# Five transposes for two token tiles, a 40-column state readout and a new hand-written order in a fused mixer kernel

## The chip, the cores and the metric

The kernel runs on 1 core of one Trainium2 chip. The metric is the device time in microseconds (us) of one execution. Before the change it is 473.45 us (median of 3 runs, 473.36 to 474.95).

## What is computed

Three blocks follow each other, for 4 batches, 768 tokens and 320 channels (8 heads of 40). The first is a gated linear-attention recurrence, done in the kernel by chunks of 128 tokens. The second is a gated convolution block. The third adds the real part of a 2-D Fourier transform, normalises each token and applies a two-layer network:

```
C = f*C + i*outer(v, k);  n = f*n + i*k          # per token, per head, 40 x 40
y = sigmoid(o) * (C @ q) / max(|n . q|, 1)
gate = sigmoid(causal_conv5(x));  x = (gate * (x @ w_val)) @ w_out
u = x + real(fft(fft(x, tokens), channels))
un = (u - mean(u)) / sqrt(var(u) + 1e-6)          # over the 320 channels of a token
out = u + relu(un @ w_ch1) @ w_ch2                # 320 -> 1280 -> 320
```

## The kernel before

The program first writes down every instruction as a unit (a run of matmuls into one output tile counts as one unit, each other instruction as its own) and then issues the units in the order of a list, `ORDER` (L44). `CELL` (L142) gives each buffer its slot, and `FILLS` (L173) puts dummy matmuls on a constant tile ahead of named units, as (unit, how many, PSUM bank). Each engine and the SP queue, which issues nearly all DMAs, works strictly in the order in which the list names its units. There is no planner at run time.

For each batch b the units come from these functions, c being one of six chunks, i one of three pairs of token tiles (one tile from each half hf of the sequence):

- `prologue_gates` (L433) and `a_fb`, `a_pre`: the gates, their decay factors d (a scan on VectorE, DVE) and the scaling of k, v and q. The gate rows are turned on TensorE (PE) with the constant `pat`, which arrives by DMA.
- `s_mm`, `u_mm` (L680), `a_u` (L693), `a_pv` (L718), `a_fin` (L754), `a_tr` (L778): scores, the state update u, the carried state cc, the read of state and values (e times cc, d times v), the division by max(|n.q|,1), and the transpose of the result. In batches 1 to 3 `a_pv` joins the scores, the e-times-cc matmuls, the u of the next chunk and the d-times-v matmuls. The first d-times-v matmul waits for an empty instruction on the SP queue, which itself waits for the last e-times-cc matmul.
- `u_mm` works in 64 x 64 quarters of the PE array: for each pair of heads p, each half chunk x and each head s, the weights are 64 columns of k from column 40h on, of which only the first 40 belong to head h. The last chunk has one x instead of two.
- `p_conv`, `p_val`, `p_g`, `p_z`, `p_fold`, `b_s`, `b_se`, `b_d` (L950), `b_de` (L961): convolution block and Fourier transform.
- `b_ln` (L980): mean and variance on DVE, the power -0.5 on GpSimd (POOL), then two ScalarE (ACT) instructions that write the two normalised tiles `un` of 320 columns. `b_ut` (L1011), called twice (L1127): three PE transposes of one tile (`tr3`, L773, columns 0 to 127, 128 to 255 and 192 to 319, so that 64 columns are turned twice), one ACT copy to `uH`, and two DVE subtractions that write the low part `uL` and the copy that lies in the other 64 partitions.
- `m_1` (L1028) and `m_2` (L1045): the two layers of the network, in 16 and 6 matmuls at a time. The low part `hl` of the hidden layer is written by DVE between them.
- Weights arrive as raw 64-bit numbers and are turned into 32-bit ones by four DVE instructions each (`to_f32`, L496, tile `mk`), in the order list spread over the work of batch 0 and the start of batch 1.

PE's list runs through batch 0 up to its normalisation, fills 23 dummy matmuls in, and then starts the first `m_1`; from there on the network of one batch stands between the attention and transform work of the next.

```
            m = slice(256 * n + 128 * q, 256 * n + 128 * q + 128)
            for k in range(2):
                ops += [(w1H[:, k, m], uH[:, k]), (w1H[:, k, m], uL[:, k]), (w1L[:, k, m], uH[:, k])]
            ops += [(w1T[:, m], uH[:, 2]), (w1U[:, m], uH[:, 2])]
```

Of the kernel before, what the change touches and what calls it, by code (L numbers as in the profile page):

```python
# [12 lines left out]
AF = mybir.ActivationFunctionType  # L13
# [25 lines left out]
NCC = 4  # L39
FB0 = 4  # L40
# [131 lines left out]
]  # L172
FILLS = [  # L173
    (78, 4, 1), (82, 8, 3), (30, 1, 0), (203, 5, 3), (262, 10, 5), (220, 2, 1), (427, 2, 1), (485, 5, 0), (512, 23,
    1), (540, 2, 1), (544, 1, 1), (1023, 2, 2),
]

# [1062 lines left out]
```

## Time and profile before

| | us |
|---|---|
| median of 3 runs | 473.45 |
| the profiled execution's own time | 474.57 |
| span of the profiled execution, first to last instruction | 472.5 |
| PE busy | 453.3 |
| DVE busy | 332.6 |
| ACT busy | 183.5 |
| POOL busy | 162.0 |

The profile gives for each engine its busy time, in 40 slices and in any stretch asked for, with the clock that PE was granted as a share of full speed (1.00 is 2.4 GHz, 0.50 is 1.2 GHz). Matmuls overlap in PE's pipeline, so the price of one in a dense run is the distance between starts, not its duration. PE weight loads (PEld) run beside the matmuls.

### The profile page before, as it was taken

To read this page: it belongs to the slowest core of one execution; us is meant where nothing else is said; L and a number is where in the kernel's file an instruction comes from. 1 tells how busy PE (TensorE), PEld (TensorE's weight loads), DVE (VectorE), ACT (ScalarE), POOL (GpSimd) and SP (SyncE) were. 2 spreads that over 40 slices of the span, in tenths; PEclk is the share of its full clock that TensorE was granted. 3 is DMA by queue.
4 is the path that set the end of the run, shared out by engine and by line. 5 is a ranking of instruction groups with operands and counts; after the bars stand their busy time and mean duration, and the time that the engine had idled before them with its cause. 6 is when DMAs were issued, how large, how long until landed. Compare 5 with 4: busy or idle time off the path is not lost.

```text
span 472.5 us, 13916 instructions
## 1 busy us (share of the span) xinstructions
PE 453.3 (96%) x5798; PEld 425.6 (90%) x5798; DVE 332.6 (70%) x810; ACT 183.5 (39%) x414; POOL 162.0 (34%) x210
## 2 busy tenths in 40 slices
PE   7998989898999989999999999999999999999996
PEld 7887767787999989889999899899999998999996
DVE  5867888899969669587568686596697683763131
ACT  5653355544334235435224254244233432342120
POOL 4554355824664331601443443122534121010000
PEclk8959999999999999999999999999999999999999
DMA  7688544634532162101330542001310000000000
GB/s 204 192 228 218 143 123 139 216 96 140 140 105 69 47 170 79 42 17 43 90 111 2 158 146 70 1 2 60 99 57 17 1 30 1 28 1 1 28 29 28
DMA packets 23301, 39.84 MB, mean 84 GB/s; under 512 B 4752, under 2 KB 14288, under 8 KB 23240
## 3 DMA queue, kind: packets, MB, share of 16 engines
q1 hardware_dynamic: 23192, 38.90, 27.6%
q8 instruction: 45, 0.74, 0.7%
q14 instruction: 16, 0.13, 0.1%
q0 software_dynamic: 48, 0.07, 0.1%
HBM read 32.77 MB, written 4.23 MB: 78 GB/s over the span
## 4 chain that ended last, share of the span: by engine, by line
PE 73%; DVE 15%; DMA 4%; ACT 3%; issue 2%; SPq 1%; POOL 1%; DVEq 0%; ACTq 0%; POOLq 0%
PE bank L300 73%; DVE mk L300 2%; DVE bank L300 2%; DVE z L300 2%; DVE d L300 2%; DMA exr<-in_c_ex_dram 1%; SPq L300 1%; DVE bs L300 1%; DMA scr<-fh 1%; DMA kvo<-in_kvo_dram 1%; DMA wvU<-tl 1%; DVE r L300 1%; DMA dmat<-in_c_d_dram 1%; DVE e L300 1%; POOL eo L300 1%
## 5 line engine op out<-in xcount | busy, mean ns | idle before, releaser
L300 PE MATMUL bank<-uu,w1H 128*128 128x256 f32 x480 | 93.2, 286 | 0.6 <-ACT gate L300 0.2
L300 PEld LDWEIGHTS bank<-uu,w1H 128*128 128x128 f32 x480 | 74.7, 188 | 2.6 <-DVE uu L300 0.8
L300 PE MATMUL bank<-w2H,hh 128*128 128x320 f32 x240 | 74.8, 319 | 0.0
L300 PE MATMUL bank<-w2L,hh 128*128 128x320 f32 x240 | 72.3, 309 | 0.0
L300 ACT ACTIVATE hh<-bank 128x512 fp32r<-128x512 f32 x60 | 35.8, 596 | 85.9 <-PE bank L300 82.7
L300 PE MATMUL bank<-uu,w1L 128*128 128x256 f32 x240 | 67.3, 281 | 0.0
L300 DVE SCALAR_TENSOR_TENSOR hl<-bank,hh 128x512 fp32r<-128x512 f32 x60 | 40.8, 686 | 27.3 <-ACT hh L300 26.6
L300 PE MATMUL bank<-w2H,hl 128*128 128x320 f32 x240 | 55.1, 310 | 1.4 <-DVE hl L300 1.4
L300 DVE SCALAR_TENSOR_TENSOR bank<-xT,cw,bank 128x384 f32<-128x384 f32 x84 | 48.3, 618 | 1.6 <-ACT bank L300 0.8
L300 PEld LDWEIGHTS bank<-w2H,hh 128*128 128x128 f32 x240 | 45.1, 188 | 1.0 <-issue 0.3
L300 PEld LDWEIGHTS bank<-w2L,hh 128*128 128x128 f32 x240 | 45.2, 188 | 0.3
L300 PEld LDWEIGHTS bank<-uu,w1L 128*128 128x128 f32 x240 | 45.2, 188 | 0.0
L300 DVE TENSOR_TENSOR z<-z,bank 128x161 f32<-128x161 f32 (+2 forms) x76 | 26.5, 377 | 21.9 <-PE bank L300 21.2
L300 PEld LDWEIGHTS bank<-w2H,hl 128*128 128x128 f32 x240 | 40.1, 188 | 1.9 <-DVE hl L300 1.9
L300 POOL TENSOR_TENSOR gL<-gg,gH 128x384 fp32r<-128x384 f32 x16 | 16.7, 1048 | 60.7 <-ACT gH L300 60.7
L300 POOL TENSOR_TENSOR cc<-cc,fcol 128x164 f32<-128x164 f32 x40 | 21.8, 544 | 36.5 <-DVE cc L300 15.7
L300 PE MATMUL bank<-uu,w1T 128*128 128x256 f32 x120 | 33.7, 281 | 0.0
L300 PE MATMUL bank<-uu,w1U 128*128 128x256 f32 x120 | 33.7, 281 | 0.0
L300 DVE TENSOR_TENSOR_SCAN d<-bank,pat 128x512 f32<-128x512 f32 x24 | 29.0, 1216 | 4.7 <-PE bank L300 4.5
L300 POOL TENSOR_TENSOR kvo<-kvo,r 128x320 f32<-128x320 f32 x24 | 17.5, 731 | 40.9 <-DVE r L300 35.3
L300 POOL TENSOR_TENSOR r<-ve,mhalf 128x2 f32<-128x2 f32 x12 | 8.3, 695 | 56.5 <-DVE ve L300 45.6
L300 POOL TENSOR_TENSOR kvo<-kvo,d 128x320 f32<-128x320 f32 x24 | 18.3, 762 | 24.5 <-DVE d L300 22.5
(153 smaller groups left out, 1047.9 us busy)
## 6 DMA issues: line engine op xcount, KB each, us to landing
kvo<-in_kvo_dram SPq DMA_DIRECT2D x24, 484.0 KB
qk<-in_qk_dram SPq DMA_DIRECT2D x48, 160.0 KB
raw<-in_w_dram SPq DMA_DIRECT2D x9, 640.0 KB
out_dram<-z SPq DMA_DIRECT2D x24, 160.0 KB
e<-sce SPq DMA_DIRECT2D x30, 80.0 KB
cs<-in_c_cs_dram SPq DMA_DIRECT2D x2, 386.0 KB
raw<-in_w_val_dram SPq DMA_DIRECT2D x1, 640.0 KB
raw<-in_w_out_dram SPq DMA_DIRECT2D x1, 640.0 KB
```

The source lines that it names most:

```text
L300: i = getattr(engine, method)(*a, **k)
```

## The change

- **Transposes.** For batches 1 to 3 the two normalised tiles of a pair are written side by side into one tile `up` of 640 columns (three ACT instructions instead of two), and five transposes of 128 columns turn all of it. The ACT copies and DVE subtractions behind it change from two and four to four and four.
- **Readout.** `u_mm` loads 40 weight columns instead of 64 and writes 40 partitions of each half instead of 64.
- **Warm-up.** The twelve dummy matmuls at the start write to six banks instead of one.
- **Order, slots and fills.** `ORDER`, `CELL` and `FILLS` are new. There are 71 dummy matmuls instead of 65.

```diff
+PAIR = (1, 2, 3)
 FILLS = [
-    (78, 4, 1), (82, 8, 3), (30, 1, 0), (203, 5, 3), (262, 10, 5), (220, 2, 1), (427, 2, 1), (485, 5, 0), (512, 23,
-    1), (540, 2, 1), (544, 1, 1), (1023, 2, 2),
+    (25, 2, 2), (45, 15, 0), (283, 5, 6), (267, 5, 6), (220, 10, 6), (427, 1, 1), (485, 3, 1), (544, 26, 3), (516, 1,
+    0), (576, 1, 6), (652, 2, 0),
 ]
...
-        for _ in range(WARM):
-            nc.tensor.matmul(out=banks()[:, 7, 0:L], lhsT=a, rhs=a, start=True, stop=True)
+        for n in range(WARM):
+            m = L * (n // 6)
+            nc.tensor.matmul(out=banks()[:, n % 6, m:m + L], lhsT=a, rhs=a, start=True, stop=True)
...
-                    T.matmul(out=u[64 * s:64 * s + 64, x, p, :], lhsT=t["kvo"][r, D * h:D * h + LS], rhs=t["vp"][r, h],
+                    T.matmul(out=u[64 * s:64 * s + D, x, p, :], lhsT=t["kvo"][r, D * h:D * h + D], rhs=t["vp"][r, h],
...
+        pair_ = wt("up", [128, 2 * DM], "U") if b in PAIR else None
+        if pair_ is not None:
+            un[b, i, "p"] = pair_
         for hf in range(2):
+            nrm = dict(scale=r0[:, hf:hf + 1], bias=nb[:, hf:hf + 1])
+            if pair_ is not None:
+                z = zt[b, hf, i]
+                for o, n in ((0, ((0, 320),)), (320, ((64, 256), (0, 64))))[hf][1]:
+                    k = (0, 320) if hf == 0 else ((0, 256) if n == 256 else (256, 320))
+                    A.activation(pair_[:, 320 * hf + o:320 * hf + o + n], z[:, k[0]:k[1]], AF.Identity, **nrm)
+                continue
             u = wt("un", [128, DM], "C")
-            A.activation(u, zt[b, hf, i], AF.Identity, scale=r0[:, hf:hf + 1], bias=nb[:, hf:hf + 1])
+            A.activation(u, zt[b, hf, i], AF.Identity, **nrm)
...
+    def b_ut2(b, i, _):
+        u = un.pop((b, i, "p"))
+        uH, uL = un[b, i]
+        for hf in range(2):
+            tp = mm("tp", [128, 3 - hf, L])
+            for j in range(3 - hf):
+                x = u[:, 384 * hf + 128 * j:384 * hf + 128 * j + 128]
+                T.matmul(out=tp[:, j, :], lhsT=x, rhs=ident, is_transpose=True, start=j == 0, stop=True,
+                         skip_group_check=True)
+            ss = slice(hf * L, hf * L + L)
+            A.activation(uH[:, 0:2, ss], tp[:, 0:2], AF.Copy)
+            V.tensor_tensor(uL[:, :, ss], tp[:, 0:2], f(uH[:, 0:2, ss]), op=ALU.subtract)
+            if hf == 0:
+                for n in range(2):
+                    r, w, sn = slice(64 * n, 64 * n + 64), slice(64 - 64 * n, 128 - 64 * n), slice(n * L, n * L + L)
+                    A.activation(uH[r, 2, sn], tp[r, 2], AF.Copy)
+                    V.tensor_tensor(uH[w, 2, sn], tp[r, 2], f(uH[r, 2, sn]), op=ALU.subtract)
```

The order list, some 2,000 numbers, is told here by its places that matter. A name such as u:0:1 is the step, the batch and the chunk (or pair); FILL15 stands for 15 dummy matmuls.

```
PE, start of the program
  before  gates FILL4 fb:0:1 fb:0:0 gates FILL8 pre:0:1 u:0:0 FILL1 gates(fm 1) fb:0:2 pre:0:0
          s0:0 gates(fm 2) u:0:1 pv:0:0 pre:0:3 pv:0:1
  after   s0:0 FILL2 gates fb:0:1 fb:0:0 fb:0:2 pre:0:1 gates(fm 1) pre:0:0 gates u:0:0 FILL15
          gates(fm 2) u:0:1 pv:0:0 pv:0:1 pre:0:2 pre:0:3
SP queue, start of the program (DMAs)
  before  gi gf qk qk pat kvo exr conv_w qk conv_w kvo qk epat conv_w conv_w kvo w_val ...
  after   gf conv_w conv_w conv_w gi conv_w qk qk pat kvo kvo epat qk w_val qk exr kvo ...
DVE, between the reciprocal and the product x of chunk 0, batch 0
  before  nothing
  after   one mk instruction, e:0:2, a reciprocal
DVE, between the two state sums cc of chunk 2, batch 0
  before  nothing
  after   one mk instruction, xH:0:0, d:0:4
PE, batch 0, normalisation to network
  before  FILL23 ut:0:0 fb:1:0 ut:0:0 FILL2 ut:0:1 FILL1 ut:0:1 m1:0:0
  after   FILL26 ut:0:1 ut:0:1 FILL1 ut:0:0 ut:0:0 s0:1 FILL1 m1:0:0
DVE, ahead of the last uu of pair 0 of batch 0: in the new order also
  the four uu of pair 1, two short steps of pair 2's normalisation, and the last of the conversion of
  one 640-column weight tile (1 instruction) and all of one 320-column tile (4 instructions)
PE, batch 1, from the first d to the first m1
  before  d:1:0 m2 d:1:2 d:1:1 fb:2:0 m2 m2 m2 m2 ut:1:0 ut:1:0 FILL2 m1:1:0
  after   d:1:0 fb:2:0 d:1:0 d:1:2 m2 m2 d:1:1 m2 s0:2 m2 ut2:1:0 (two tiles) ut2:1:0 (three) fb:2:1 m1:1:0
SP queue, batch 1, just ahead of the empty instruction of chunk 4
  before  gate rows, out, k/v/o of batch 3 chunk 4, out
  after   out, e, e, qk, qk, out, gate rows
```

## Rows read from the trace of the kernel before

**Rows 1.** Page, parts 1 and 2: busy us and share; granted clock in 40 slices.

```profile
PE 453.3 (96%) x5798; PEld 425.6 (90%) x5798; DVE 332.6 (70%) x810; ACT 183.5 (39%) x414; POOL 162.0 (34%) x210
...
PEclk8959999999999999999999999999999999999999
```

**Rows 2.** Windows: from:to, length, then busy us and count per engine, clock, DMA.

```profile
0.00:22.50 22.50, 18.31 (x270) 16.97 (x272) 15.50 (x30) 13.93 (x27) 12.80 (x21) 0.92 0.68 194
22.50:35.50 13.00, 12.74 (x235) 11.65 (x230) 9.14 (x24) 7.40 (x24) 6.18 (x8) 0.50 0.80 233
35.50:47.00 11.50, 9.88 (x209) 8.97 (x208) 9.00 (x19) 4.18 (x12) 5.50 (x8) 0.95 0.86 221
47.00:107.50 60.50, 55.83 (x593) 46.02 (x592) 53.72 (x138) 30.16 (x69) 30.44 (x33) 0.98 0.47 140
107.50:168.00 60.50, 57.71 (x1006) 55.23 (x1007) 49.51 (x100) 22.34 (x45) 29.95 (x33) 1.00 0.36 107
168.00:468.50 300.50, 298.53 (x3499) 286.76 (x3497) 195.21 (x501) 105.53 (x241) 77.08 (x108) 1.00 0.16 49
```

**Rows 3.** Waits of PE from 107.5 us on: us in total, times, longest.

```profile
PE bank L300 <- DVE hl L300: 1.5, 2, 1.4
PE bank L300 <- SPq L304: 1.0, 1, 1.0
```

**Rows 4.** Timeline of PE: start, us; runs of nine and of three transposes of un.

```profile
421.22 1.15 PE L300 MATMUL bank<-pat,un 128*128 128x128 f32 x9
...
432.03 0.49 PE L300 MATMUL bank<-pat,un 128*128 128x128 f32 x3
```

**Rows 5.** Timeline of PE, batch 2: e times cc, u, d times v.

```profile
234.24 0.63 PE L300 MATMUL bank<-cc,e 40*64 40x41 f32 x32
234.68 0.66 PE L300 MATMUL bank<-kvo 64*64 64x41 f32 x32
235.15 0.66 PE L300 MATMUL bank<-kvo,d 64*64 64x41 f32 x32
...
266.55 0.66 PE L300 MATMUL bank<-kvo 64*64 64x41 f32 x16
```

**Rows 6.** Groups of weight loads by form: busy us, mean ns, idle before.

```profile
L300 PEld LDWEIGHTS bank<-cs,eo 128*128 128x128 f32 x64 | 10.4, 189 | 2.0 <-POOL eo L300 1.1 <-issue 0.8
...
L300 PEld LDWEIGHTS bank<-cs,eo 128*64 128x64 f32 x64 | 5.0, 136 | 1.3 <-issue 0.5 <-ACT kvo L300 0.2 <-DVE os L300 0.2
```

**Rows 7.** Timeline of ACT and PE, batch 1, pair 0: un, transposes, first m1.

```profile
208.56 1.20 ACT L300 ACTIVATE un<-z,nb,r 128x320 f32<-128x320 f32 x2 [1.53 <-DVE nb L300]
209.85 1.04 ACT L300 ACTIVATE uu<-bank 128x384 fp32r<-128x384 f32 x2
...
209.26 1.09 PE L300 MATMUL bank<-pat,un 128*128 128x128 f32 x6
...
210.94 0.84 PE L300 MATMUL bank<-uu,w1H 128*128 128x256 f32 x2
```

**Rows 8.** Timeline of DVE: its two longest waits, 22 to 47 us.

```profile
29.42 0.49 DVE L300 TENSOR_TENSOR x<-bank,kvo 128x320 f32<-128x320 f32 x1 [2.20 <-POOL kvo L300]
...
39.82 0.33 DVE L300 TENSOR_TENSOR cc<-cc,bank 128x164 f32<-128x164 f32 x1 [2.04 <-POOL cc L300]
```

**Rows 9.** Groups of DVE by form: conversions mk and split uu; busy us, mean ns.

```profile
L300 DVE SCALAR_TENSOR_TENSOR mk<-raw,mk 128x640 int32<-128x640 int32 x22 | 19.0, 862 | 0.2
...
L300 DVE TENSOR_TENSOR uu<-bank,uu 128x256 fp32r<-128x256 f32 x24 | 10.0, 420 | 5.3 <-ACT uu L300 5.1
...
L300 DVE TENSOR_TENSOR uu<-bank,uu 64x128 fp32r<-64x128 f32 x24 | 6.6, 291 | 1.3 <-ACT uu L300 0.9
...
L300 DVE SCALAR_TENSOR_TENSOR mk<-raw,mk 128x320 int32<-128x320 int32 x6 | 4.2, 700 | 0.1
```

**Rows 10.** Timeline of PE: its waits for pat and for the second fm, batch 0.

```profile
7.89 0.28 PE L300 MATMUL bank<-pat,gi 32*128 32x32 f32 x2 [1.97 <-DMA pat<-in_c_pat_dram]
...
21.38 0.48 PE L300 MATMUL bank<-fm,epat 32*128 32x128 f32 x2 [1.17 <-DVE fm L300]
```

More of the change, by code (lines that the diff above doesn't have):

```diff
@@ L1125, in mixer_kernel @@
             run("ln", b_ln, b, i)
-            for hf in range(2):
+            if b in PAIR:
+                run("ut", b_ut2, b, i, 0)
+            for hf in range(0 if b in PAIR else 2):
                 run("ut", b_ut, b, i, hf)
```

251 rows, old and new, of tables (CELL, ORDER) are left out of this document.

## The prediction

> **What bounds the kernel now.** I read the page first and then cut the span into stages by windows. PE is busy 96% of the span and DVE 70% [rows 1], but that is an average over two regimes. From 168 us on PE is busy 298.53 of 300.50 us while DVE is busy 195.21; there only PE's own work counts, and at most 1.97 us of gaps can be won [rows 2]. From 107.5 to 168 us PE lacks 60.50 - 57.71 = 2.79 us; the waits that end there are one for DVE's `hl` (1.4 of 1.5 us) and one for the empty SP instruction (1.0 us) [rows 3]. Before 107.5 us, where the first network matmul of batch 0 starts, DVE sets the pace: from 47 us it is busy 53.72 of 60.50 us. In the first 47 us it is idle 7.00 + 3.86 + 2.50 = 13.4 us, waiting for DMAs, POOL and a PE that had half its clock from 22.5 to 35.5 us [rows 2]. PE's busy time there says little, since dummy matmuls count as busy.
>
> So the end of the program is the start of the first `m_1` (107.5 us), plus PE's work after it, plus PE's gaps after it. I cost the change by these three. The profiled run took 474.57 us, 2.1 more than its span and 1.1 more than the median of 473.45; the sum is made against 474.57.
>
> **Transposes.** Nine pairs lose one transpose each. Nine in a row take 1.15 us and three take 0.49, so one costs (1.15 - 0.49) / 6 = 0.11 us [rows 4]. All nine lie in the PE-bound stage: 9 x 0.11 = -1.0 us. If a change of operand eats as much as it frees the gain is 0, and it can't be over 1.0. ACT gets one more normalising instruction and two more copies per pair; ACT is busy 105.53 of 300.50 us there [rows 2], so their work is hidden, except where PE waits for the pair, below. DVE keeps four subtractions.
>
> **Readout.** A group of 32 u-instructions starts 0.47 us before the next kind of matmul, and a group of 16, which uses two of the four quarters of the array, takes the same 0.66 us from start to end [rows 5]. So the pace is set by the quarter: 0.47 us / 8 = 0.058 us for each slot of a quarter, not by the number of instructions. That the slot is the weight load is likely from the loads of one operand: 128 columns take 189 ns, 64 take 136, which is 0.83 ns a column [rows 6]. Twenty-four columns fewer are then 20 ns a slot and 8 x 20 = 0.16 us a group. Batches 1 to 3 have 18 groups: at most -2.9 us, at least 0. But 15 of them are what PE does while the SP queue answers the wait ahead of d times v; a shorter group uncovers part of it. I take 0.10 us a group, -1.8 us. Batch 0's groups lie in the DVE-paced stage and give nothing.
>
> The trace paces these matmuls at 0.47 / 32 = 15 ns. The Trainium skill (TensorE: Matmul & The Clock Gate, "Wait — 56ns, not 53.3ns?") says that starts never come closer than about 25 ns however narrow the matmul; by that rule fewer columns would give nothing at all. The trace contradicts the figure, but a floor of its own close to 15 ns isn't excluded, and that case is a rival.
>
> **The pair's chain in batch 1.** Now the first `un` is ready at about 209.2 us, the transposes start at 209.26 and the first `m_1` at 210.94 [rows 7]. In the new order the first transposes are those of the second tile, which need two of the three ACT instructions, and the last three need all: 1.20 us of ACT plus a short third one, instead of 0.6. The PE work between the first `d` and these transposes is a little less than now, and behind them only one `fb` matmul stands ahead of `m_1`, with the copies and subtractions in between (1.04 us of ACT for both tiles now, rows 7). I take +1.2 us, once; from 0 to +2.1. In batches 2 and 3 the lists put one to three `m_2` groups behind the transposes, which cover it.
>
> **Gaps after 107.5 us.** Together they are 4.8 us. The SP wait of 1.0 us goes, because in the new order the output DMA that stood right ahead of the empty instruction, and the DVE step that it waits for, have been moved up. Of the `hl` wait I let half go: conversions that DVE did between the first `uu` and the first `hl` now stand before, but others come in. I take -1.5; the bounds are -4.8 and, as a new list can open gaps of its own, +2.
>
> **The start, to the first `m_1`.** DVE must do more before it: four `uu` of pair 1 (2 x 0.42 + 2 x 0.29 = 1.42), one `mk` of 640 columns (0.86) and the conversion of a 320-column tile (2 x 0.70 and two shorter), at least 3.7 us [rows 9]. Against that, DVE's two longest stalls are given work: between the reciprocal and x (2.20 us, behind POOL) and between two state sums (2.04 us, behind POOL) stand now other DVE steps [rows 8]. That is -4.2. FILL15 keeps PE busy during the wait for the second `fm` (1.17 us), after which PE fell to half its clock for 13 us [rows 10, 2]; with full clock the rest of DVE's 6.4 idle us from 22.5 to 47 could go too. On the other side `pat` goes from fifth to ninth place in the SP queue, and PE already waits 1.97 us for it [rows 10]; the FILL4 that now follows it is gone, so I let these cancel. I take -0.5; from -6.4 + 3.7 = -2.7 to +3.7.
>
> The longer block of dummy matmuls ahead of the transposes (26 for 23) costs nothing as long as DVE's chain is later than PE. The warm-up's six banks cost nothing: the matmuls are the same and PE runs them in order. All other moves of the lists are taken as inside the bounds above.
>
> **Sum.** -1.0 - 1.8 + 1.2 - 1.5 - 0.5 = -3.6 us: 471.0 for an execution like the profiled one, 469.8 at the median.
>
> **The rivals.** *PE keeps its clock at the start.* All 6.4 us of DVE idle go, and most gaps and the whole readout gain come: -1.0 - 2.9 + 1.2 - 3.5 - 2.7 = -8.9, 464.6. For it speaks FILL15 at the very place where PE fell idle; against it, that from 22.5 to 35.5 us the DMA engines are 80% busy too [rows 2]. *The readout gives nothing*, by a floor on starts: 469.8 + 1.8 = 471.6, inside 0.5%. For it: no row shows a quarter-array matmul with fewer weight columns than 64, so a floor just below 15 ns would stay unseen; against it, as far as the trace goes: the group of 16 that takes as long as the group of 32 [rows 5]. *The gains cancel*: the stalls at the start go but the gaps stay, and batch 1 costs 2.1: 473.45 - 1.0 - 1.8 + 2.1 - 0.5 = 472.3. *Slower: the first layer starts late.* The mechanism is DVE's queue ahead of the first `m_1`. If the two POOL stalls come back elsewhere in the first 47 us, the 3.7 us stand, PE idles behind them, and the later gaps don't close because DVE owes the same sum by the end of batch 1: 473.45 + 3.7 - 1.0 - 1.0 + 1.2 = 476.4 us. It decides from the point where less than 1.5 of the 4.2 us of stalls is won. For it speaks that DVE's sum ahead of that point is surely larger; against, that the same conversions no longer stand between the first `uu` and the first `hl`.
>
> **How the numbers follow.** Forecast 0.40, clock kept 0.15, readout nothing 0.12, gains cancel 0.15, slower 0.18. A measurement tells this kernel from no change at about 0.5%, 2.4 us: below 471.1 is faster, above 475.8 slower. That gives faster 0.55, same 0.27, slower 0.18. The range of 8 in 10 runs from the clock case with its own spread, 463.5, up to the slower case, 476.0.
>
> **What would show it.** Transposes of the pairs fall from 54 to 45 at an unchanged 0.11 us. The u group should start 0.30 to 0.37 us before d times v instead of 0.47. The windows should give a first `m_1` between 105 and 108 us; a start beyond 110 us with DVE idle in the first 47 us still over 12 us would be the slower case. A granted clock of 1.00 from 22 to 36 us would be the faster one. The wait for the empty SP instruction should be gone; if it appears 15 times at 0.1 us, the readout uncovered it. In batch 1, PE should be idle for about 1 us ahead of the pair's first `m_1`. I would be wrong if PE's gaps after 168 us grew beyond 2 us, or if the first layer's start moved by more than 4 us either way.

## The result and the profile after

The changed kernel takes 477.45 us (median of 14 runs, 475.78 to 482.94), the kernel before 473.81 us in runs on the same chip: a ratio of 1.0059, 95% interval 1.0030 to 1.0087. It is slower by 0.6%. The forecast was 469.8 us, with 463.5 to 476.0 as range, so the prediction was wrong in sign and the time lies outside the range. The ratios and their intervals are taken from fast runs alone (the 482.94 was a slow one), so they aren't the quotients of the medians. The profiled execution of the changed kernel took 478.08 us.

The first rows are from the page of the changed kernel (busy us, share, count; clock in 40 slices), to be read against [rows 1]. PE is busy 4 us less than before and the span is 3.6 us longer: the parts have taken work off PE, and idle time has taken its place.

```profile
PE 449.3 (94%) x5801; PEld 421.5 (89%) x5801; DVE 327.3 (69%) x810; ACT 187.3 (39%) x441; POOL 159.5 (34%) x210
...
PEclk8887999999999999999999989999999999999999
```

The windows of the changed kernel, over the stretches of [rows 2] (from:to, length, busy us and count of PE, PEld, DVE, ACT, POOL, then clock, DMA share, GB/s):

```profile
0.00:22.50 22.50, 18.98 (x242) 17.95 (x242) 16.19 (x31) 13.03 (x23) 11.60 (x19) 0.85 0.68 199
22.50:35.50 13.00, 8.72 (x261) 7.60 (x259) 8.23 (x22) 5.29 (x15) 8.13 (x11) 0.88 0.67 205
35.50:47.00 11.50, 10.11 (x195) 8.93 (x195) 8.85 (x17) 4.70 (x14) 6.05 (x8) 0.69 0.72 205
47.00:107.50 60.50, 54.99 (x599) 46.38 (x600) 51.79 (x134) 30.29 (x74) 28.81 (x33) 1.00 0.56 158
107.50:168.00 60.50, 58.62 (x926) 55.93 (x925) 46.79 (x107) 24.70 (x53) 25.47 (x31) 1.00 0.33 99
168.00:468.50 300.50, 294.11 (x3562) 281.16 (x3561) 194.49 (x502) 109.26 (x266) 79.49 (x112) 0.99 0.16 48
```

Two losses stand here. The first `m1` of batch 0 starts at 112.40 us instead of 107.54, with a little more work done by then; what that is worth is taken up behind the experiments. And from 168 us on PE was idle 1.97 us before [rows 2] and is idle 6.39 us now. PE's waits in that stretch name the places (us in total, times, longest):

```profile
PE bank L302 <- POOL kvo L302: 2.2, 1, 2.2
PE bank L302 <- ACT xT L302: 1.4, 1, 1.4
PE bank L302 <- ACT uu L302: 0.8, 1, 0.8
PE bank L302 <- DVE nb L302: 0.6, 1, 0.6
```

**The wait of 1.4 us.** SP, ACT and PE around 248 us (start, us, engine, instruction, in brackets the idle time before it and what ended it):

```profile
243.82 0.36 SPq L302 DMA_DIRECT2D kvo<-in_kvo_dram  x1
...
247.89 0.47 ACT L302 ACTIVATE kvo<-kvo 128x320 f32<-128x320 f32 x1 [2.80 <-DMA kvo<-in_kvo_dram]
248.27 0.47 ACT L302 ACTIVATE xT<-bank 128x384 f32<-128x384 f32 x1
...
248.79 0.50 PE L302 MATMUL bank<-uu,w1H 128*128 128x256 f32 x2 [1.42 <-ACT xT L302]
```

SP issues the load of k, v and o of chunk 5 of batch 2 at 243.82 us. ACT's sigmoid of that chunk waits for it until 247.89, 2.80 us in which ACT has other work but may not start it: the copy `xT` of an earlier chunk stands behind the sigmoid in ACT's list. PE's next `m1` is to use the bank that `xT` reads. So PE waits for a load that no matmul near it needs.

**The wait of 2.2 us.** The same on POOL, 25 us later:

```profile
266.92 0.36 SPq L302 DMA_DIRECT2D kvo<-in_kvo_dram  x1
...
270.79 1.27 POOL L302 TENSOR_TENSOR e<-e,qk 128x512 f32<-128x512 f32 x1 [2.26 <-DMA e<-sce]
272.39 0.73 POOL L302 TENSOR_TENSOR kvo<-kvo,isT 128x328 f32<-128x328 f32 x1 [0.34 <-DMA kvo<-in_kvo_dram]
273.09 0.73 POOL L302 TENSOR_TENSOR kvo<-kvo,d 128x320 f32<-128x320 f32 x1
...
273.88 0.46 PE L302 MATMUL bank<-kvo 64*40 64x41 f32 x13 [2.21 <-POOL kvo L302]
```

The instruction for which PE waits is the product of `kvo` and `d` at 273.09, chunk 5 of batch 2. Ahead of it on POOL stand a product for the row tile `e` of that chunk, which waited 2.26 us for its own DMA, and a scaling by `isT` that belongs to chunk 2 of batch 3 and whose load was issued at 266.92. PE needs neither yet.

Finer windows show the stage where this falls. Of the kernel before, then of the changed one:

```profile
205.00:240.00 35.00, 34.59 (x520) 32.66 (x519) 26.14 (x80) 12.00 (x25) 11.70 (x18) 1.00 0.21 64
240.00:264.00 24.00, 24.00 (x392) 23.16 (x391) 18.42 (x38) 8.66 (x19) 8.42 (x12) 1.00 0.21 68
264.00:290.00 26.00, 25.11 (x331) 24.14 (x330) 19.02 (x41) 11.95 (x28) 10.62 (x13) 1.00 0.45 140
```

```profile
205.00:240.00 35.00, 33.74 (x513) 31.23 (x512) 26.93 (x84) 14.27 (x37) 10.40 (x16) 1.00 0.16 45
240.00:264.00 24.00, 22.58 (x355) 21.67 (x357) 16.85 (x35) 8.76 (x19) 5.52 (x8) 1.00 0.11 37
264.00:290.00 26.00, 23.68 (x363) 22.68 (x351) 14.93 (x35) 8.58 (x22) 9.22 (x12) 0.93 0.48 138
```

From 205 to 290 us PE's idle time goes from 1.30 to 5.00 us. And behind the 2.2 us wait the granted clock is 0.93 over 26 us, where it was 1.00; at 0.07 of the stretch that is another 1.8 us at most.

### The profile page after: what moved, and what is told of

Same layout as the page of the kernel before. It is cut to its first block, busy times and chain, and to the rows that moved or that the text cites. A ratio compares the mean times of both kernels' runs of the same rounds, so it can differ in the third digit from the quotient of the medians.

```text
span 476.1 us, 13939 instructions
## 1 busy us (share of the span) xinstructions
PE 449.3 (94%) x5801; PEld 421.5 (89%) x5801; DVE 327.3 (69%) x810; ACT 187.3 (39%) x441; POOL 159.5 (34%) x210
## 4 chain that ended last, share of the span: by engine, by line
PE 78%; DVE 9%; DMA 5%; issue 2%; ACT 2%; POOL 1%; SPq 1%; DVEq 0%; ACTq 0%; POOLq 0%
PE bank L302 77%; DMA kvo<-in_kvo_dram 3%; DMA qk<-in_qk_dram 2%; SPq L302 1%; PE bank L358 1%; DVE z L302 1%; DVE d L302 1%; DVE bank L302 1%; DVE uu L302 1%; POOL eo L302 1%; DVE bs L302 1%; POOL kvo L302 1%; DVE mk L302 1%; ACT uu L302 1%; DVE x L302 0%
## 5 line engine op out<-in xcount | busy, mean ns | idle before, releaser
L302 POOL TENSOR_TENSOR cc<-cc,fcol 128x164 f32<-128x164 f32 x40 | 20.6, 514 | 44.5 <-DVE cc L302 21.6
L302 POOL TENSOR_TENSOR kvo<-kvo,isT 128x328 f32<-128x328 f32 x24 | 18.4, 771 | 25.7 <-DMA kvo<-in_kvo_dram 22.6
```

The lines of the kernel that those rows point to most:

```text
L302: i = getattr(engine, method)(*a, **k)
```

## The experiments

Steps are named as in the order list above; u:2:4 is step u of batch 2, chunk 4. Each ratio is to runs of the kernel before on the same chip.

The theories were: **A**, the parts gain and the new order loses it at the start, where the first `m1` came at 112.4 instead of 107.5 us; **B**, it is lost in batch 2, at the two waits; **C**, the parts themselves gain nothing or cost.

### Each part in the old order, and the old start

**e1**: the kernel before with the 40-column readout and the six-bank warm-up.

```diff
-                    T.matmul(out=u[64 * s:64 * s + 64, x, p, :], lhsT=t["kvo"][r, D * h:D * h + LS], rhs=t["vp"][r, h],
+                    T.matmul(out=u[64 * s:64 * s + D, x, p, :], lhsT=t["kvo"][r, D * h:D * h + D], rhs=t["vp"][r, h],
```

> The kernel before with the 40-column readout (and the warm-up over six banks that it needs) and nothing else: order, buffers and fills as they were. Theory A (the two parts gain what was forecast, the new order of the start loses more): about 1.8 us less than the kernel before, 472.0 us at its median of 473.8. Theory C (the narrower readout gains nothing, since the starts of those matmuls have a floor): within 0.5 us of the kernel before.

Measured: 473.67 us, ratio 0.9970 (0.9939 to 1.0000). A gain of 0.3%, between the two theories, with an interval that just reaches no gain. Its trace shows a place where some of it was lost again. PE and SP of e1 at 165 us, and the window behind:

```profile
164.86 0.75 SPq L300 DMA_DIRECT2D out_dram<-z  x1
...
165.72 0.68 PE L300 MATMUL bank<-kvo,d 64*64 64x41 f32 x32 [1.61 <-SPq L304]
...
166.00:176.00 10.00, 9.84 (x138) 9.39 (x131) 5.24 (x15) 3.09 (x8) 3.85 (x5) 0.83 0.48 144
```

The output store in the first line stands on SP right ahead of the empty instruction for which PE waits. That wait, 1.0 us before [rows 3], has grown to 1.61, and the clock of the next 10 us is 0.83. This was followed up in e11 and e14.

**e2** and **e3**: five transposes in the old order, each step of a pair where the old steps stood; e2 with 64 columns, e3 with 40.

```diff
-PE   ut:b:i:0 (three transposes)  ut:b:i:1 (three)      ACT  un un  uu uu
+PE   ut2:b:i (three)  ut2:b:i (two)                     ACT  up up up  uu uu uu uu
```

> The kernel before with five instead of six transposes in batches 1 to 3 and nothing else: each step of a pair stands where the old steps stood, and the readout keeps 64 columns. Theory A: 1.0 us less for nine transposes and up to 1.2 us more where the first pair of batch 1 waits for both of its normalisations, so 472.8 to 474.0 us beside 473.8. Theory C: 474 us or more, since the transposes lie beside waits and two more evictions by ACT and one more subtraction by DVE come on each pair.

> Both parts in the old order, with the old fills and, but for 20 buffers, the old buffers. Theory A: the sum of the two, 471.0 to 472.2 us beside 473.8, so some 5 to 6 us less than the changed kernel. Theory B (the parts and the start matter little; the late loads of batch 2 lose it): about 473.8 less 1 to 2 us as well, so this run tells only the parts' own worth. Theory C: 474 us or more.

Measured: 484.57 us, ratio 1.0209 (1.0177 to 1.0241), and 482.41 us, ratio 1.0160 (1.0124 to 1.0197). Both lie above the 474 us of theory C, and by far more than its reasons give. PE's waits from 168 us on in e2:

```profile
PE bank L306 <- DVE uu L306: 5.3, 5, 1.9
```

Five waits for DVE's subtractions. In the longest, the first `m1` of batch 1 was to write a bank that the last subtraction of the pair had just read; the new slots had been handed out without regard to that. So these two runs don't price the pairs; e10 and e13 repeat them.

**e4**: the changed kernel, but everything up to the transforms of batch 1 issued in the order of the kernel before, with its fills and slots there.

```diff
-ORDER  new order
+ORDER  the first 956 steps of the old order, then all others as the new order has them
```

> The changed kernel, with all that it has, but its work up to the transforms of batch 1 (about 205 us) is issued in the order of the kernel before; from there on in its own order. Theory A (the start loses 3.5 to 4.9 us: the first m1 at 112.4 instead of 107.5 us): 472.5 to 474 us, first m1 back at 107 to 108 us. Theory B (what is lost is lost in batch 2, where two loads come late and PE stands 1.4 and 2.2 us with a lower clock behind; an earlier start is waited away there): 476 to 477.5 us, near the changed kernel's 477.45, with both waits still there and longer.

Measured: 490.01 us, ratio 1.0310 (1.0270 to 1.0350). Both theories missed: beside the two waits (1.85 and 1.73 us here) a third came, 5.35 us ahead of the transform of batch 2. It is of their kind:

```profile
302.90 0.99 SPq L306 DMA_DIRECT2D kvo<-in_kvo_dram  x2
...
309.36 0.83 ACT L306 ACTIVATE kvo<-kvo 128x320 f32<-128x320 f32 x2 [3.53 <-DMA kvo<-in_kvo_dram]
...
312.63 1.90 PE L306 MATMUL bank<-dmat,w 128*1 128x161 f32 x5 [5.35 <-DVE w L306]
```

ACT's copies `od` stand behind two sigmoids, which wait 3.53 us for loads issued at 302.90; DVE's `w` waits for `od`, and PE for `w`. One line of e4 speaks on theory A. The first `m1` of the pair of batch 1, in e4 and then in the changed kernel:

```profile
214.41 0.85 PE L306 MATMUL bank<-uu,w1H 128*128 128x256 f32 x2 [0.80 <-ACT uu L306]
```

```profile
214.41 0.84 PE L302 MATMUL bank<-uu,w1H 128*128 128x256 f32 x2 [0.81 <-ACT uu L302]
```

The old start brought batch 1 no sooner to this point, by which both have issued the same matmuls but for the dummies. In e4 the first `m1` came at 108.0 us, 4.4 sooner, but from there PE was idle 4.9 us instead of 2.0, and it had more left to do: ahead of its first `m1` the new order has also issued the scores and the state update of one chunk (64 matmuls, 1.0 us). These are single executions, and the start varies. The same start list in the changed kernel, in e5 and in e9 (below):

```profile
112.40 0.47 PE L302 MATMUL bank<-uu,w1H 128*128 128x256 f32 x2 [0.31 <-DVE uu L302]
```

```profile
109.41 0.47 PE L306 MATMUL bank<-uu,w1H 128*128 128x256 f32 x2 [0.32 <-DVE uu L306]
...
112.72 0.47 PE L306 MATMUL bank<-uu,w1H 128*128 128x256 f32 x2 [0.32 <-DVE uu L306]
```

Over all profiles, the seven profiles of the new start list have it between 109.4 and 113.6 us, 111.5 on average, and the nine of the old list between 106.1 and 109.6, 107.5 on average.

### Steps that wait for late loads, and the parts in the new order

**e5**: the changed kernel with four steps issued later on their engines.

```diff
 ACT
-xH:2:1  sigmoid:2:5  xT:2:1  hh:1:1:1  xH:2:2  xT:2:2
+xH:2:1  xT:2:1  hh:1:1:1  xH:2:2  xT:2:2  sigmoid:2:5
-sigmoid:3:2  hh:1:2:2
+hh:1:2:2  sigmoid:3:2
 POOL
-cc:2:3  isT:2:5  cc:2:4  fin:2:2
+cc:2:3  cc:2:4  fin:2:2  isT:2:5
-e:2:4  e:2:5  isT:3:2  d:2:5  cc:2:5  fin:2:4
+e:2:4  e:2:5  d:2:5  cc:2:5  fin:2:4  isT:3:2
```

> The changed kernel with four of its steps issued later on their engines and nothing else: the gate scaling by POOL and the sigmoid by ACT of chunk 5 of batch 2, and the same two of chunk 2 of batch 3, go behind the steps that stood behind them and for which PE waits (at 248.8 and 273.9 us), since each of the four waits for a load that is issued late. Theory B (what was lost was lost in batch 2, by these two waits of 1.4 and 2.2 us and the lower clock behind them): 472.5 to 474 us beside the changed kernel's 477.45, and no PE wait over 0.5 us between 245 and 285 us. Theory C (the five transposes cost it, wherever they stand): 476 us or more.

Measured: 473.99 us, ratio 0.9987 (0.9948 to 1.0026), 3.5 us below the changed kernel. The first wait is gone. Of the second, 1.40 us were left, since the other step in front of the product stayed:

```profile
266.49 1.27 POOL L306 TENSOR_TENSOR e<-e,qk 128x512 f32<-128x512 f32 x1 [2.70 <-DMA e<-sce]
267.72 0.74 POOL L306 TENSOR_TENSOR kvo<-kvo,d 128x320 f32<-128x320 f32 x1
...
268.51 0.46 PE L306 MATMUL bank<-kvo 64*40 64x41 f32 x13 [1.40 <-POOL kvo L306]
```

**e9**: e5 and two more moves, the second in the pair of batch 1 (copies of the five transposes: block 0 and 1 of the first tile last, now second).

```diff
 POOL
-e:2:4  e:2:5  d:2:5  cc:2:5  fin:2:4  isT:3:2
+e:2:4  d:2:5  cc:2:5  e:2:5  fin:2:4  isT:3:2
 ACT, ut2:1:0
-uu (second tile)  uu (64 columns)  uu (64 columns)  uu (first tile)
+uu (second tile)  uu (first tile)  uu (64 columns)  uu (64 columns)
```

> The run with the four steps moved, and two more: POOL's product for the row tile of chunk 5 of batch 2 goes behind the two POOL steps for which PE still waited 1.4 us at 268.5 us, and in the first pair of batch 1 ACT copies the first two blocks of the five transposes second instead of last, so that PE's first m1 need not wait 0.8 us at 211.5 us for them. Theory B (single steps standing ahead of others in an engine's queue): 471.5 to 473 us, both waits under 0.4 us. If PE is then held by the next step in the chain: 474 us as before.

Measured: 472.61 us, ratio 0.9952 (0.9922 to 0.9981). Windows of e9:

```profile
205.00:240.00 35.00, 33.77 (x513) 31.28 (x512) 27.23 (x84) 13.92 (x37) 10.25 (x16) 1.00 0.15 44
240.00:264.00 24.00, 24.00 (x397) 23.30 (x397) 17.62 (x37) 9.02 (x20) 6.94 (x10) 1.00 0.14 45
264.00:290.00 26.00, 25.89 (x341) 25.09 (x340) 19.37 (x45) 11.93 (x27) 9.22 (x13) 1.00 0.45 137
```

Both waits are gone, PE's idle time from 205 to 290 us is 1.34 us, as before the change, and the clock is 1.00 again. Its profiled execution took 472.56 us, 5.5 less than that of the changed kernel, with a first `m1` that came even later (112.72 us). Six steps out of 2,023 turn the change from 0.6% slower to 0.5% faster. Theory B stands, as the reason for the change of sign. The sixth move gave nothing that shows: the wait ahead of the `m1` of batch 1 went from 0.81 us for ACT to 0.26 and 0.51 us for DVE.

**e7**: the changed kernel with 64 readout columns again (the diff of e1 backwards).

> The changed kernel with the readout of 64 columns again and nothing else. If the narrower readout is worth in this order what it was in the old one (474.68 to 473.67 us, ratio 0.997): 478.5 to 479.2 us, 1.0 to 1.8 us above the changed kernel. If it is worth nothing where PE waits for loads anyway: 477.5 us.

Measured: 481.29 us, ratio 1.0133 (1.0079 to 1.0187), so the readout is worth 0.7% here, 3.5 us, more than expected; the two intervals, 1.0030 to 1.0087 and this, overlap a little.

**e6** and **e8**: six transposes again in the new order (the diff of e2 backwards), without and with the four moves of e5.

> The changed kernel with six transposes again in batches 1 to 3: each old step stands where the step of the pair stood in the new order; the readout keeps 40 columns. Theory C (the chain of three normalisations, five transposes, four copies and four subtractions costs more than nine transposes save): 474 to 476 us, the wait of 0.8 us ahead of the first m1 of batch 1 gone. Theory B (the pairs save their 1.0 us and the loss is in the loads): 478 to 479 us.

> Six transposes again and the four steps moved, in the new order with 40 columns. If both matter and they are independent: the sum of the two runs' gains, 469 to 472 us, below the kernel before. If what PE is given back in batch 1 is waited for in batch 2: no better than the better of the two.

Measured: 482.49 us, ratio 1.0172 (1.0120 to 1.0224), and 476.42 us, ratio 1.0037 (0.9999 to 1.0075). Both miss: e6 is beyond the numbers of both theories, and e8, with no gain from e6 to add, is no faster than e5. The four moves are worth 1.35% here, and 0.72% with five transposes. Six transposes came out slower than five, but in e6 again with a bank that had just been left: PE waits 2.25 us for a subtraction ahead of the first `m1` of batch 1. e12 repeats this without it.

### What the parts are worth by themselves

**e11**: e1 with three SP transfers behind the d-times-v product of chunk 4 of batch 1. **e14**: the same move alone, in the kernel before.

```diff
 SP queue, batch 1
-out:0:1  kvo:3:4  out:0:1  (empty instruction of pv:1:4)
+(empty instruction of pv:1:4)  out:0:1  kvo:3:4  out:0:1
```

> The kernel before with the 40-column readout, and three transfers of SP (two output stores of batch 0 and one load of batch 3) issued behind the product d times v of chunk 4 of batch 1 instead of ahead of it. In the run with the readout alone, PE waited 1.6 us there for an empty instruction that stood behind these three on SP, which themselves waited for a sum of DVE, and the granted clock of the 10 us behind was 0.83. Theory E (what the readout gained in batch 1 was lost at that wait): 471 to 472.5 us, the wait under 0.2 us and a clock of 1.00 from 166 to 176 us. If the wait is for something else: 473.7 us as before.

> The kernel before with 64 columns and its own order, with only the three transfers of SP behind the product of chunk 4 of batch 1. The wait there is 1.0 us in the kernel before and its clock stays at 1.00, so if the move is worth that wait alone: 1.0 us less, a ratio of 0.998; the readout then has the rest of the 0.9921 that both together gave. If the move alone gives 0.994 or less, the readout is worth little in the old order.

Measured: e11 471.02 us, ratio 0.9921 (0.9891 to 0.9952), the fastest of all; e14 472.93 us, ratio 0.9956 (0.9929 to 0.9983). In both the wait is gone; in e11 the clock is back:

```profile
166.00:176.00 10.00, 9.84 (x125) 9.31 (x124) 6.16 (x17) 4.94 (x14) 4.12 (x5) 1.00 0.78 205
```

So theory E holds, though e14 lies between its two expectations, and the move is worth 0.44% even without the readout. That is 2.1 us for a wait of 1.0, more than the wait explains; the interval, 0.8 to 3.4 us, leaves room. What the readout adds is 0.9956 to 0.9921, 0.35% or 1.7 us, and 0.30% or 1.4 us in e1.

**e10**: e3 with the copies that the first `m1` reads in front and no `m1` in a bank just freed. **e13**: the same on top of e11, and no filler in such a bank either.

```diff
 ACT, e10 and e13, ut2:b:i
-uu (first tile)  uu (64)  uu (64)  uu (second tile)
+uu (first tile)  uu (second tile)  uu (64)  uu (64)
```

> Both parts in the old order once more, as in the run of 482.41 us, but placed better: the copies and subtractions of a pair that the first m1 reads first come first, and an m1 gets no bank that was freed just before by a pair's last subtraction. Theory D (the 8 to 9 us that the pairs cost in the old order were the places of their steps and the banks handed on, not the pairs): 472 to 475 us, the waits of 1.9, 1.1 and 1.3 us ahead of m1 and of the spreading of gates gone. Theory C (the longer chain itself): 479 us or more.

> The fastest run so far (the old order, 40 columns, three transfers behind the product) with five transposes in batches 1 to 3; the copies that the first m1 reads come first, no m1 and no filler gets a bank that a pair's subtraction has just freed. Theory C (the longer chain of a pair is on the path where the order leaves no other work for PE): 473 to 476 us beside 471.02, the wait ahead of the first m1 of batch 1 at 1 us or more. Theory D (places and banks alone): 470 to 471.5 us.

Measured: e10 478.01 us, ratio 1.0081 (1.0055 to 1.0107), between the two theories; a filler ahead of the first `m1` waited 1.77 us for a subtraction. e13 474.12 us, ratio 0.9996 (0.9964 to 1.0028), 0.75% slower than e11, as theory C has it, though the wait ahead of the first `m1` is a little under the 1 us expected:

```profile
210.57 0.39 PE L306 MATMUL bank<-uu,w1H 128*128 128x256 f32 x1 [0.91 <-DVE uu L306]
```

**e12**: e9's POOL and ACT moves in batch 2, with six transposes, subtractions straight behind copies and no `m1` in a bank that a transpose just left.

```diff
-PE   ut2:b:i (three)  ut2:b:i (two)                     ACT  up up up  uu uu uu uu
+PE   ut:b:i:0 (three transposes)  ut:b:i:1 (three)      ACT  un un  uu uu
```

> The new order with 40 columns and with the moved steps of POOL and ACT in batch 2, but with six transposes again in batches 1 to 3, their subtractions straight behind their copies and no m1 in a bank that a transpose has just left. Theory C (the pairs cost more than they save, also in the order that was made for them): 469 to 471 us, below the 472.61 us of the run with six moved steps. Theory A (nine transposes of 0.11 us are saved, the longer chain is hidden in this order): 473.3 to 474.5 us.

Measured: 476.22 us, ratio 1.0028 (0.9994 to 1.0062), 0.76% slower than e9 and slower than either theory had it. It has waits of its own, for DVE's subtractions:

```profile
PE bank L305 <- DVE uu L305: 2.9, 3, 1.3
```

In the old order the pairs cost 3.5 us, in the new one they are worth 3.6, each with some 2 us of uncertainty. Each order was laid out for its own steps, and the steps that were put in later find places that don't fit. What five transposes are worth with an order of their own in both cases stays open.

## Why the prediction was wrong

**Transposes, -1.0: right in PE's work.** There are 45 for the pairs instead of 54 (72 with the 18 of batch 0), at the old price: in a dense run they still start 0.11 us apart. The groups by form (count, busy us, mean ns) of the kernel before and of the changed one:

```profile
L300 PE MATMUL bank<-pat,un 128*128 128x128 f32 x72 | 11.4, 280 | 0.6 <-ACT un L300 0.5
```

```profile
L302 PE MATMUL bank<-pat,up 128*128 128x128 f32 x45 | 7.6, 279 | 0.7 <-DVE nb L302 0.6
```

**Readout, -1.8: right, and somewhat low.** The timeline of the changed kernel, to be held against [rows 5]:

```profile
242.63 0.63 PE L302 MATMUL bank<-cc,e 40*64 40x41 f32 x32
243.07 0.53 PE L302 MATMUL bank<-kvo 64*40 64x41 f32 x32
243.41 0.68 PE L302 MATMUL bank<-kvo,d 64*64 64x41 f32 x32
...
263.73 0.50 PE L302 MATMUL bank<-kvo 64*40 64x41 f32 x32
264.04 0.67 PE L302 MATMUL bank<-kvo,d 64*64 64x41 f32 x32
```

The group starts 0.34 and 0.31 us ahead of d times v, instead of 0.47: 0.13 to 0.16 us saved, the upper end of the bounds, where 0.10 was taken; over 18 groups that is 2.3 to 2.9 us of PE's work. In the old order the measured time fell by 1.4 and 1.7 us. The slot of a quarter shrinks with its weight columns, by about the 20 ns that were worked out from [rows 6]; that the load itself is the slot stays argued, since the outputs were narrowed with it. The uncovering of SP's answer came once, with 0.6 us in e1, not 15 times. The rival of a floor on starts is out.

**The pair's chain in batch 1, +1.2: right.** 0.81 us of PE's waiting, in bounds.

**The start, -0.5: this step failed.** The stretch up to the first `m1`, of the kernel before and the changed one:

```profile
0.00:107.54 107.54, 96.77 (x1296) 83.62 (x1296) 87.39 (x209) 55.67 (x129) 54.92 (x69) 0.90 0.60 171
...
0.00:112.40 112.40, 96.29 (x1371) 83.36 (x1372) 89.81 (x220) 57.33 (x132) 56.62 (x71) 0.92 0.59 170
```

It came 4.9 us later, of which 1.0 is work brought forward. DVE's busy time ahead of it grew by 2.4 us (at least 3.7 was counted), but its idle time grew too, from 20.2 to 22.6 us, where stalls of 4.2 us were to be won. That is the slower rival's mechanism, with both of its signs: 112.4 is beyond 110, and DVE was idle 13.7 us in the first 47, over the 12. What the new start costs by itself no run shows, since e4 changed more; the averages of the profiles, 111.5 and 107.5, speak for about 3 us beside the work brought forward. Theory A is true in part. Why DVE's idle time grew stays open. Of the fill that was to keep the clock, 22.5 to 35.5 us went from 0.50 to 0.88, but 35.5 to 47 from 0.95 to 0.69.

**Gaps, -1.5: this step failed too, and it turned the sign.** The gaps after the first `m1` were 4.8 us, were to be 3.3, and are 6.9 (0.46 up to 168 us, 6.39 behind). The SP wait went, and of `hl` 0.8 of 1.5 us are left, as was said. But "a new list can open gaps of its own, +2" was a bound, not a count; the two gaps that it opened in batch 2 cost 3.6 us and the clock behind them up to 1.8. The prediction followed the new lists from the start to the pair of batch 1 and there stopped. This loss stands 35 to 60 us further on, in the orders of ACT and POOL, and they could have been read from the same lists: a step that waits for a load just issued, with a step ahead of PE behind it. The prediction had named this sign too: PE's gaps after 168 us grew beyond 2 us, to 6.39.

**The sum.** The prediction adds up the first `m1`, PE's work behind it and PE's gaps behind it. The stretch from the first `m1` to PE's last matmul, in the kernel before, the changed one and e9:

```profile
107.54:468.77 361.23, 356.51 (x4503) 342.00 (x4503) 244.69 (x601) 127.87 (x285) 107.03 (x141) 1.00 0.19 59
...
112.40:472.29 359.89, 353.04 (x4430) 338.12 (x4430) 237.01 (x590) 129.94 (x309) 102.93 (x140) 1.00 0.19 57
...
112.72:466.92 354.20, 351.34 (x4430) 336.72 (x4430) 237.50 (x590) 129.87 (x309) 102.67 (x140) 1.00 0.19 58
```

| us against the kernel before | forecast | changed kernel | e9 |
|---|---|---|---|
| first `m1` | -0.5 | +4.9 | +5.2 |
| PE's work behind it | -2.8 | -3.5 | -5.2 |
| PE's gaps behind it | -0.3 | +2.1 | -1.9 |
| sum | -3.6 | +3.5 | -1.9 |

The forecast of -0.3 is -1.5 and the pair's +1.2. In both measured columns 1.0 us of work has moved from the second row into the first. With the six places put right the change gives 0.9952 (0.9922 to 0.9981), where the forecast, 469.8 of 473.45, is 0.9923. That the two are so near is partly luck: e9 starts as late as the changed kernel, and fewer gaps and a readout worth more than forecast make up for part of it. The slower rival's 476.4 us is luck in part as well: it has the late start, but lets the old gaps stand and knows nothing of the new ones, and it takes 1.0 for the readout where the forecast takes 1.8. The range ended at 476.0, below that rival.

## What to carry to other kernels

When an order is written by hand, go through each engine's list for steps that need a fresh load and ask what stands behind them: a step for a later batch costs nothing where it waits, but everything behind it on its engine waits too, and PE waits for that, also by way of a bank that a copy has yet to read or of a store that stands in a DMA queue. A step that is taken from one order and put into another brings its own stalls (0.75% here, either way), so the worth of a part and the worth of its order can't be told apart by swapping alone. Compare two orders by PE's idle time and clock, stage by stage; the time at which a named step starts says something only beside the work that each order has issued by then, and over several executions.

## What the runs showed that was not expected

- **Starts 10 ns apart.** 32 matmuls with 40 weight columns on quarters of the array start within 0.31 to 0.34 us, 10 ns each, where those with 64 take 15 [rows 5]. The Trainium skill (TensorE: Matmul & The Clock Gate, "Wait — 56ns, not 53.3ns?") says that starts are never closer than about 25 ns; with the starts of all four quarters counted together the trace disagrees. On one quarter they are about 40 ns apart (8 in 0.31 to 0.34 us), so for a single quarter nothing here contradicts it.
- **A wait can cost more than its length.** After 1.61 us of idling in e1 the granted clock was 0.83 over 10 us, with 0.50 (1.2 GHz) from 168 to 170 us; after 1.40 us in e5 it was 0.83 from 265 to 275 us, and after 2.21 us in the changed kernel 0.93 over 26. The length alone doesn't decide: after 1.04 us in the kernel before, 1.42 us in the changed kernel and 1.85 us in e4 it stayed at 1.00.
- **The start varies from execution to execution.** The same list reached the first `m1` at 109.4, 112.4 and 112.7 us.
